# A change to the first stage of a causal-attention and gated feed-forward kernel: a small constant, two low halves, column sums and transposes are placed elsewhere

## The chip, the cores and the metric

One core of one Trainium2 chip. The metric is the device time of one execution in microseconds. Below, TensorE is PE in the rows (PEld is its weight load), VectorE DVE, ScalarE ACT, GpSimd POOL and SyncE SP.

## What is computed

Causal attention over 4 batches, 12 heads, 448 positions and a head width of 64, then an RMS norm and a gated feed-forward layer over the 1792 tokens (768 columns, 1536 inner columns), all in float32:

```python
scores = np.where(mask, -1e9, q @ k.T / sqrt(64))
attn = np.exp(scores - np.max(scores, axis=-1, keepdims=True))
attn = attn / (np.sum(attn, axis=-1, keepdims=True) + 1e-09)
x = (attn @ v)                       # heads side by side: 1792 x 768
xn = x / np.sqrt(np.mean(x * x, axis=-1, keepdims=True) + 1e-06) * rms_g
g = xn @ w_gate
out = (g * sigmoid(g) * (xn @ w_val)) @ w_out
```

## The kernel before, in words

The tokens are handled in three groups. The work of attention comes in units: one pair of heads, and 256 queries for the first group. The first group has 12 units (`ENDS[0]`), two for each of the six chunks c of 128 columns of x. This first stage, some 60 us, is where everything below happens; later stages do the same for the other groups while the feed-forward layer of the group before runs on TensorE.

Every matrix product of the feed-forward layer is made of three matmuls in a short float format: weights and x are split into a high half (ScalarE's cast, `w_h` in L456, `xh` in L362) and a low half (what the cast left off, `w_l` in L458 on VectorE or through `pool_op`, L105, on GpSimd; `xl` in L363). A weight chunk is such a triple on one column chunk: L502, L503, L504. Weight tiles arrive as 64-bit words and are converted first: ScalarE in L443, then VectorE in L444 and L446.

The order on each engine is the order in which the program is written; each engine works its queue strictly in turn. The program is written tick by tick: `round_steps(p)` gives six steps for round p, and each step is a tick. Scores of unit p + 3 (`DP`), products of unit p and transposes of unit p + 1 belong to round p. `post(delay, f)` puts f so many ticks later; the delays stand in the table `T`. `LOAD`, `CONVERT` and `SPLIT` give the ticks at which weight tiles 0 to 7 are loaded, converted and split, and `READY_W`, `READY_X` those from which weight chunks may be woven in.

For one unit: scores on TensorE (L195), row minimum and mask on VectorE (L204), exponentials with their row sums on ScalarE (L207, four of them), the constant 1e-9 added to the sums on ScalarE (L229), reciprocal on VectorE (L216), the rows scaled on GpSimd (L212, four instructions; on ScalarE in L210 for the last unit), transposes on TensorE in two halves e = 0 and 1 (L251), their copies to SBUF (L255 on VectorE, L257 on ScalarE), products with v (L280).

After the second unit of a chunk: the split of x, and its squares on ScalarE (L318). The tile `sq` has one buffer; chunks 1 to 4 are added on GpSimd into `acc` (L105). For the last chunk the sum over columns is made by `column_sums` on TensorE: first of `acc`, then of `sq`, into the same bank (L371, four matmuls of one column each time). `rms_first` then makes the square root on ScalarE (L380), the reciprocal and four diagonal blocks on VectorE (L383, L385), and a matmul that spreads them (L389), copied on ScalarE (L390). The first eviction of a product (L519) needs that. The stage ends with the scores of the next group (`refill`).

## Time and profile before

| | us |
|---|---|
| median of 3 runs (669.01 to 669.62) | 669.44 |
| the profiled execution | 670.19 |
| its span, first to last instruction | 668.4 |
| TensorE busy (98% of the span) | 657.7 |
| VectorE busy (77%) | 515.3 |
| ScalarE busy (54%) | 360.9 |
| GpSimd busy (44%) | 291.3 |

The shares are means over stages that differ much. Three views tell of the first stage: busy time by stretch, the chain of waits (the work that ended last, followed back from the end, in order of time), and each engine's instructions in order of time. In the last, an instruction's duration can be longer than the time till the next one starts, since they overlap a little.

### The profile page before, as it was taken

To read this page: it belongs to the slowest core of one execution; us is meant where nothing else is said; L and a number is where in the kernel's file an instruction comes from. 1 tells how busy PE (TensorE), PEld (TensorE's weight loads), DVE (VectorE), ACT (ScalarE), POOL (GpSimd) and SP (SyncE) were. 2 spreads that over 40 slices of the span, in tenths; PEclk is the share of its full clock that TensorE was granted. 3 is DMA by queue.
4 is the path that set the end of the run, shared out by engine and by line. 5 is a ranking of instruction groups with operands and counts; after the bars stand their busy time and mean duration, and the time that the engine had idled before them with its cause. 6 is when DMAs were issued, how large, how long until landed. Compare 5 with 4: busy or idle time off the path is not lost.

```text
span 668.4 us, 11848 instructions
## 1 busy us (share of the span) xinstructions
PE 657.7 (98%) x4122; PEld 551.7 (83%) x4122; DVE 515.3 (77%) x1049; ACT 360.9 (54%) x801; POOL 291.3 (44%) x278
## 2 busy tenths in 40 slices
PE   9899999999999999999999999999999999999997
PEld 6567877778777777777777778888899999999997
DVE  5997987889876776778778885496776866889992
ACT  6996866766866445454454444435424343355540
POOL 4670313245344365766767475643424342502220
PEclk9999999999999999999999999999999999999999
DMA  8876888898696375866757555235576467562641
GB/s 258 288 254 217 252 284 266 257 293 244 220 353 234 118 218 192 272 203 222 239 190 253 167 180 181 91 112 187 206 245 190 155 210 236 196 173 69 179 143 60
DMA packets 71357, 138.81 MB, mean 208 GB/s; under 512 B 7745, under 2 KB 39233, under 8 KB 71297
## 3 DMA queue, kind: packets, MB, share of 16 engines
q1 hardware_dynamic: 71296, 138.05, 63.4%
q8 instruction: 33, 0.54, 0.3%
q14 instruction: 28, 0.22, 0.1%
HBM read 104.21 MB, written 33.82 MB: 206 GB/s over the span
## 4 chain that ended last, share of the span: by engine, by line
PE 86%; ACT 5%; DVE 3%; DMA 3%; issue 2%; POOL 1%; SPq 0%; DVEq 0%; ACTq 0%
PE m_ps L502 14%; PE m_ps L504 14%; PE m_ps L503 13%; PE s_ps L652 9%; PE m_ps L652 8%; PE a_ps L280 6%; PE t_ps L251 5%; PE y_ps L652 5%; PE x_ps L652 4%; PE s_ps L195 4%; PE x_ps L195 2%; ACT sp L207 2%; DMA w<-in_w 1%; DVE a_l L545 1%; DMA v_r<-in_v 1%
## 5 line engine op out<-in xcount | busy, mean ns | idle before, releaser
L212 POOL TENSOR_SCALAR sp<-sp,rs 128x384 f32<-128x384 f32 (+3 forms) x164 | 122.9, 769 | 164.0 <-DVE rs L216 151.1
L502 PE MATMUL m_ps<-xh,w_h 128*128 128x512 f32 x276 | 116.8, 423 | 0.0
L207 ACT ACTIVATE sp<-sp,nm 128x128 f32<-128x128 f32 (+3 forms) x168 | 87.1, 522 | 42.8 <-DVE nm L204 42.8
L504 PE MATMUL m_ps<-xh,w_l 128*128 128x512 f32 x276 | 108.5, 393 | 0.0
L503 PE MATMUL m_ps<-xl,w_h 128*128 128x512 f32 x276 | 108.0, 391 | 0.0
L105 POOL TENSOR_TENSOR a_l<-w_q,a_h 128x768 fp32r<-128x768 f32 x24 | 48.2, 2010 | 82.4 <-ACT a_h L543 81.0
L255 DVE COPY pt<-t_ps 128x384 f32<-128x384 f32 (+1 forms) x79 | 46.7, 591 | 24.1 <-PE t_ps L251 23.7
L504 PEld LDWEIGHTS m_ps<-xh,w_l 128*128 128x128 f32 x276 | 51.8, 188 | 11.6
L502 PEld LDWEIGHTS m_ps<-xh,w_h 128*128 128x128 f32 x276 | 51.9, 188 | 11.3 <-issue 3.0
L105 POOL TENSOR_TENSOR w_l<-w_r,w_h 128x768 fp32r<-128x768 f32 x30 | 57.6, 1926 | 6.3 <-ACT w_h L456 6.0
L503 PEld LDWEIGHTS m_ps<-xl,w_h 128*128 128x128 f32 x276 | 52.2, 189 | 8.1 <-issue 0.2
L502 PE MATMUL m_ps<-hh,w_h 128*128 128x512 f32 x144 | 58.1, 403 | 0.0
L251 PE MATMUL t_ps<-ident,sp 128*128 128x128 f32 (+1 forms) x348 | 56.5, 274 | 0.6 <-ACT pt L257 0.5
L251 PEld LDWEIGHTS t_ps<-ident,sp 128*128 128x128 f32 (+1 forms) x348 | 42.9, 138 | 16.5 <-issue 2.4
L504 PE MATMUL m_ps<-hh,w_l 128*128 128x512 f32 x144 | 56.2, 390 | 0.0
L503 PE MATMUL m_ps<-hl,w_h 128*128 128x512 f32 x144 | 56.1, 390 | 0.0
L280 PEld LDWEIGHTS a_ps<-pt,v_r 128*64 128x64 f32 (+1 forms) x816 | 37.2, 137 | 19.7 <-issue 8.4
L204 DVE CUSTOM_DVE_ANT_0 sp<-s_ps,mask 128x128 f32<-128x128 f32 (+2 forms) x114 | 42.6, 422 | 11.1 <-PE s_ps L195 9.7
L280 PE MATMUL a_ps<-pt,v_r 112*64 112x64 f32 (+2 forms) x816 | 47.3, 262 | 1.4 <-DVE pt L255 1.2
L543 ACT CAST a_h<-w_q 128x768 fp32r<-128x768 f32 (+1 forms) x48 | 35.0, 753 | 13.2 <-DMA w_q<-wz 4.9
L105 POOL TENSOR_TENSOR acc<-acc,sq 128x384 f32<-128x384 f32 (+1 forms) x19 | 22.5, 1185 | 39.5 <-ACT sq L340 36.7
L458 DVE TENSOR_TENSOR w_l<-w_c,w_h 128x768 fp32r<-128x768 f32 x36 | 37.5, 1042 | 0.6 <-ACT w_h L456 0.5
(196 smaller groups left out, 1620.5 us busy)
## 6 DMA issues: line engine op xcount, KB each, us to landing
w<-in_w SPq DMA_DIRECT2D x36, 768.0 KB, 5.1
w<-w_c SPq DMA_DIRECT2D x36, 384.0 KB, 5.6
w_r<-w SPq DMA_DIRECT2D x36, 384.0 KB, 4.6
qk_r<-in_qk SPq DMA_DIRECT2D x48, 256.0 KB, 4.4
qk_r<-in_qk SPq DMA_DIRECT2D x12, 512.0 KB, 6.4
v_r<-in_v SPq DMA_DIRECT2D x12, 448.0 KB, 4.2
v_r<-in_v SPq DMA_DIRECT2D x24, 192.0 KB, 3.0
wy<-w_r SPq DMA_DIRECT2D x24, 192.0 KB, 3.9
```

What stands on the lines that cost most here:

```text
L105: nc.gpsimd.tensor_tensor(out_, a, b, op=op)
L195: nc.tensor.matmul(ps, r[:, q0: q0 + nq], r[:, k0: k0 + wd], start=True, stop=True)
L204: nc.vector.tensor_tensor_reduce(out=sp, in0=ps, in1=mk, scale=nsc, scalar=3.0e38, op0=ALU.add, op1=ALU.min, accum_out=nm)
L207: post(T["exp" if p >= ENDS[0] else "exp0"], lambda: nc.scalar.activation(sp, sp, AF.Exp, bias=nm, scale=-1.0, accum_out=sm))
L212: pr["norms"].append(lambda: nc.gpsimd.tensor_scalar(sp, sp, rs, 1.0, op0=ALU.mult, op1=ALU.mult))
L251: nc.tensor.transpose(ps[:kb, at: at + P], pr["sp"][e][:, o + kb * j: o + kb * (j + 1)], ident)
L255: nc.vector.tensor_copy(pt[:kb, :at], ps[:kb, :at])
L280: nc.tensor.matmul(at_[e * D: (e + 1) * D, p % 2, q0: q0 + n], raw_v[p][:kb, h, j, e, :], pr["pt", e][:kb, a0: a0 + n], start=(j == 0), st ...
L502: nc.tensor.matmul(ps, wh[:, k, :], mh, start=(first and k == ks[0]), stop=False)
L503: nc.tensor.matmul(ps, wh[:, k, :], ml, start=False, stop=False)
L504: nc.tensor.matmul(ps, wl[:, k, :], mh, start=False, stop=(last and k == 5))
L652: nc.tensor.matmul(ps, a[x], b[y], start=first and n == 0, stop=last and n == 2, skip_group_check=True)
```

## The change

Five edits, all in the first stage:

- The constant 1e-9 is added to the row sums on VectorE, just ahead of the reciprocal, for the first 12 units; ScalarE's addition (L229) stays for later ones.
- The copy of the first half of the transposes (e = 0) goes to VectorE for units 0, 2, 4, 6, 8 rather than for units 0, 1, 3, 4, 6, 7, 9; the others go to ScalarE.
- The last chunk's squares are added into `acc` by VectorE, and `column_sums` runs once, three ticks after the squares rather than one (`r0`).
- The low halves of weight tiles 0 and 1 are made by GpSimd rather than VectorE.
- In the last round that still makes scores (p = 8) both halves of the transposes follow each other, rather than three ticks apart.

```diff
-         ld=4, ld1=11, lv=2, norm0=7, norm=6, norm1=2, r0=1, sq=1, ...
+         ld=4, ld1=11, lv=2, norm0=7, norm=6, norm1=2, r0=3, sq=1, ...
         def norm():
+            if p < ENDS[0]:
+                nc.vector.tensor_scalar_add(pr["sm"][:, :nb], pr["sm"][:, :nb], 1e-9)
             nc.vector.reciprocal(pr["rs"][:, :nb], pr["sm"][:, :nb])
...
-            post(T["exp" if p >= ENDS[0] else "exp0"], lambda: nc.scalar.activation(
-                pr["sm"][:, :nb], pr["sm"][:, :nb], AF.Identity, bias=tiny))
+            if p >= ENDS[0]:
+                post(T["exp"], lambda: nc.scalar.activation(
+                    pr["sm"][:, :nb], pr["sm"][:, :nb], AF.Identity, bias=tiny))
...
-            if kind or p < ENDS[0] and (e or p % 3 < 2 and p < 10):
+            if kind or p < ENDS[0] and (e or p % 2 == 0 and p < 10):
                 nc.vector.tensor_copy(pt[:kb, :at], ps[:kb, :at])
...
         def squares():
-            if last:
-                cols = column_sums(acc[0, 0], None, True)
             nc.scalar.activation(sq, x, AF.Square)
             if last:
-                post(T["r0"], lambda: rms_first(column_sums(sq, cols, False)))
+                nc.vector.tensor_tensor(acc[0, 0], acc[0, 0], sq, op=ALU.add)
+                post(T["r0"], lambda: rms_first(column_sums(acc[0, 0])))
...
-                             start=first and i == 0, stop=not first, skip_group_check=True)
+                             start=True, stop=True)
...
-            if s < NU or s > NU + 2 * NF and s % 2:
+            if 1 < s < NU or s > NU + 2 * NF and s % 2:
...
-        if s_:
+        if s_ and p + DP < ENDS[0] - 1:
             return [scores, products, ts[0]] + 2 * noop + ts[1:]
```

What this does to the order at three places. On VectorE, at the end of the first stage, from the last low halves of x (`xl`) to the first eviction (`gr`); `rc` is the reciprocal root, `dg` the diagonal blocks, `w_c` a converted weight tile. Before:

```order
L363 SCALAR_TENSOR_TENSOR xl<-a_ps,g_sb,xh 128x512
L363 SCALAR_TENSOR_TENSOR xl<-y_ps,g_sb,xh 128x512
L383 RECIPROCAL rc<-rc 128x4
L385 TENSOR_SCALAR dg<-ident,rc 128x128 x4
L444 TENSOR_SCALAR w_717<-w_717 128x768
L446 SCALAR_TENSOR_TENSOR w_c<-w_c,w_717 128x768
L444 TENSOR_SCALAR w_820<-w_820 128x768
L446 SCALAR_TENSOR_TENSOR w_c<-w_c,w_820 128x768
L519 TENSOR_TENSOR gr<-m_ps,rms 128x512
```

After:

```order
L365 SCALAR_TENSOR_TENSOR xl<-a_ps,g_sb,xh 128x512
L321 TENSOR_TENSOR acc<-acc,sq 128x512
L365 SCALAR_TENSOR_TENSOR xl<-y_ps,g_sb,xh 128x512
L446 TENSOR_SCALAR w_716<-w_716 128x768
L448 SCALAR_TENSOR_TENSOR w_c<-w_c,w_716 128x768
L446 TENSOR_SCALAR w_819<-w_819 128x768
L448 SCALAR_TENSOR_TENSOR w_c<-w_c,w_819 128x768
L385 RECIPROCAL rc<-rc 128x4
L387 TENSOR_SCALAR dg<-ident,rc 128x128 x4
L521 TENSOR_TENSOR gr<-m_ps,rms 128x512
```

The addition of the squares is new, and the four instructions of the weight conversions now stand ahead of the reciprocal and the diagonal blocks.

On TensorE, at the same place, from the last column sums (`t_ps<-ones`) to the spread (`t_ps<-dg`). Before:

```order
L371 MATMUL t_ps<-ones,sq 128x1 x4
L502 MATMUL m_ps<-xh,w_h 128x512
L503 MATMUL m_ps<-xl,w_h 128x512
L504 MATMUL m_ps<-xh,w_l 128x512
L502 MATMUL m_ps<-xh,w_h 128x512
L503 MATMUL m_ps<-xl,w_h 128x512
L504 MATMUL m_ps<-xh,w_l 128x512
L502 MATMUL s_ps<-xh,w_h 128x512
L503 MATMUL s_ps<-xl,w_h 128x512
L504 MATMUL s_ps<-xh,w_l 128x512
L389 MATMUL t_ps<-dg,ones 128x512
```

After:

```order
L373 MATMUL t_ps<-ones,acc 128x1 x4
L504 MATMUL s_ps<-xh,w_h 128x512
L505 MATMUL s_ps<-xl,w_h 128x512
L506 MATMUL s_ps<-xh,w_l 128x512
L391 MATMUL t_ps<-dg,ones 128x512
```

Two of the three weight chunks between the sums and the spread now stand ahead of the sums.

On GpSimd, in the middle of the stage, from the end of unit 6's scaling over unit 7's (`sp_531`, `sp_532` before, `sp_530`, `sp_531` after) to the addition of chunk 1's squares. Before:

```order
L212 TENSOR_SCALAR sp_476<-sp_476,rs_474 128x256
L212 TENSOR_SCALAR sp_531<-sp_531,rs_530 128x128
L212 TENSOR_SCALAR sp_531<-sp_531,rs_530 128x256
L212 TENSOR_SCALAR sp_532<-sp_532,rs_530 128x128
L212 TENSOR_SCALAR sp_532<-sp_532,rs_530 128x256
L105 TENSOR_TENSOR acc_406<-acc_406,sq_515 128x512
```

After:

```order
L212 TENSOR_SCALAR sp_476<-sp_476,rs_474 128x256
L105 TENSOR_TENSOR w_l_573<-w_c_399,w_h_572 128x768
L212 TENSOR_SCALAR sp_530<-sp_530,rs_529 128x128
L212 TENSOR_SCALAR sp_530<-sp_530,rs_529 128x256
L212 TENSOR_SCALAR sp_531<-sp_531,rs_529 128x128
L212 TENSOR_SCALAR sp_531<-sp_531,rs_529 128x256
L105 TENSOR_TENSOR acc_405<-acc_405,sq_515 128x512
```

The low half of weight tile 1 stands between unit 6's scaling and unit 7's; that of tile 0 stands likewise between units 4 and 5.

## Rows read from the trace of the kernel before

**Rows 1.** The page's first part: busy us (share) x instructions.

```profile
PE 657.7 (98%) x4122; PEld 551.7 (83%) x4122; DVE 515.3 (77%) x1049; ACT 360.9 (54%) x801; POOL 291.3 (44%) x278
```

**Rows 2.** Busy time by stretch: length, engines, granted clock, DMA share, GB/s.

```profile
17.00:30.00 13.00, 11.07 (x83) 7.46 (x82) 11.70 (x46) 12.87 (x44) 8.26 (x14) 1.00 0.78 279
30.00:43.00 13.00, 12.38 (x87) 8.38 (x85) 12.75 (x43) 12.48 (x40) 10.97 (x15) 1.00 0.80 274
43.00:50.30 7.30, 6.71 (x42) 4.74 (x42) 5.72 (x10) 7.24 (x20) 3.91 (x6) 1.00 0.74 250
50.30:60.00 9.70, 9.70 (x53) 7.60 (x53) 6.13 (x12) 6.01 (x10) 0.00 (x0) 1.00 0.50 177
60.00:80.00 20.00, 20.00 (x96) 15.84 (x96) 19.27 (x41) 15.47 (x35) 4.22 (x4) 1.00 0.80 264
...
663.00:668.40 5.40, 1.84 (x11) 1.53 (x9) 0.56 (x1) 0.00 (x0) 0.00 (x0) 0.95 0.20 73
```

**Rows 3.** The chain of waits, 27 to 35 us: start, us, what.

```profile
27.76 0.37 ACT pt L257
...
29.88 0.02 issue
29.91 0.30 ACT sm L229
30.20 0.73 ACT w_h L456
30.93 2.37 POOL sp L212 x3
33.30 1.27 POOL acc L105
...
34.59 0.60 ACT sq L318
```

**Rows 4.** Groups by line and shape, 17 to 50 us: busy us, mean ns, idle before.

```profile
L229 ACT ACTIVATE sm<-sm,tiny 128x4 f32<-128x4 f32 x8 | 2.4, 298 | 0.3
...
L216 DVE RECIPROCAL rs<-sm 128x4 f32<-128x4 f32 x8 | 1.4, 172 | 1.6 <-ACT sm L229 1.5
```

**Rows 5.** The same view of the whole span, GpSimd: low halves of later weight tiles.

```profile
L105 POOL TENSOR_TENSOR w_l<-w_r,w_h 128x768 fp32r<-128x768 f32 x30 | 57.6, 1926 | 6.3 <-ACT w_h L456 6.0
```

**Rows 6.** GpSimd in order of time: start, us, first shape of four instructions.

```profile
9.19 1.64 POOL L212 TENSOR_SCALAR sp<-sp,rs 128x128 f32<-128x128 f32 x4 [6.42 <-DVE rs L216]
...
30.58 2.72 POOL L212 TENSOR_SCALAR sp<-sp,rs 128x128 f32<-128x128 f32 x4 [0.99 <-DVE rs L216]
```

**Rows 7.** TensorE in order of time; each fp32 matmul counts twice.

```profile
50.26 0.87 PE L280 MATMUL y_ps<-pt,v_r 128*64 128x256 f32 x8 [0.18 <-ACT pt L257]
51.06 1.05 PE L371 MATMUL t_ps<-ones,acc 128*128 128x1 f32 x8
...
55.72 1.02 PE L389 MATMUL t_ps<-dg,ones 128*128 128x512 f32 x2
...
60.12 0.37 PE L195 MATMUL s_ps<-qk_r 64*128 64x128 f32 x1
```

**Rows 8.** ScalarE in order of time: the last chunk's squares.

```profile
51.70 0.58 ACT L318 ACTIVATE sq<-y_ps 128x512 f32<-128x512 f32 x1
```

**Rows 9.** VectorE in order of time: a conversion at 41.41, then the stage's end.

```profile
41.41 1.48 DVE L446 SCALAR_TENSOR_TENSOR w_c<-w_c,w 128x768 int32<-128x768 int32 x1
...
52.89 0.75 DVE L363 SCALAR_TENSOR_TENSOR xl<-y_ps,g_sb,xh 128x512 fp32r<-128x512 f32 x1 [2.96 <-ACT xh L362]
54.03 0.18 DVE L383 RECIPROCAL rc<-rc 128x4 f32<-128x4 f32 x1 [0.39 <-ACT rc L380]
...
55.13 0.56 DVE L444 TENSOR_SCALAR w<-w 128x768 int32<-128x768 int32 x1
...
57.19 0.96 DVE L446 SCALAR_TENSOR_TENSOR w_c<-w_c,w 128x768 int32<-128x768 int32 x1
58.07 0.68 DVE L519 TENSOR_TENSOR gr<-m_ps,rms 128x512 f32<-128x512 f32 x1
```

More of the change, by code (lines that the diff above doesn't have):

```diff
@@ L46 @@
 T = dict(c0=0, c2=4, c20=16, c3=4, c30=18, c26=5, c36=5, c5=6, c50=19, c56=7, exp=1, exp0=3, gt=1, hh=1, hl=4, ws=5, ld2=7,
-         ld=4, ld1=11, lv=2, norm0=7, norm=6, norm1=2, r0=1, sq=1, acc=10, acc4=7, dg=1, spread=3, r1=5, so=3, wl=2, wl0=8, wl2=5, wl4=1, xl=2, xl0=9)
+         ld=4, ld1=11, lv=2, norm0=7, norm=6, norm1=2, r0=3, sq=1, acc=10, acc4=7, dg=1, spread=3, r1=5, so=3, wl=2, wl0=8, wl2=5, wl4=1, xl=2, xl0=9)
 LOAD = (1, 15, 27, 37, 48, 60, 72, 84)
@@ L365, in x_split, with column_sums @@
         xh[b, c], xl[b, c] = h, l
-    def column_sums(sq, ps, first):
-        ps = bank("t")[:, : W // P] if first else ps
+    def column_sums(sq):
+        ps = bank("t")[:, : W // P]
         for i in range(W // P):
             nc.tensor.matmul(ps[:, i: i + 1], sq[:, P * i: P * (i + 1)], ones[:, :1],
-                             start=first and i == 0, stop=not first, skip_group_check=True)
+                             start=True, stop=True)
         return ps
```

## The prediction

> **What bounds the kernel now.** I read the page's first part, then busy time by stretch. TensorE is busy 98% of the span [rows 1]. From 60 us on it has no gap to speak of: 20.00 of 20.00 us in the first stretch behind the first stage [rows 2]. So what delays or advances TensorE before 60 us moves the end by as much, unless a later stretch takes it back. The change lies wholly before 60 us. There, from 30 to 43 us, VectorE (12.75 of 13.00), ScalarE (12.48) and GpSimd (10.97) are all nearly full, and TensorE has small gaps [rows 2]. The chain of waits in that stretch runs over ScalarE, except where it goes to GpSimd: ScalarE casts the high half of weight tile 1 until 30.93, GpSimd scales the rows of unit 7 and adds the squares of chunk 1 to the running sum, and only at 34.59 can ScalarE take the next square, since the tile `sq` has one buffer [rows 3]. From 50.3 to 60 us TensorE is full (9.70 of 9.70) [rows 2]: it alternates column sums, the matmul that spreads 1/rms, and weight chunks of three matmuls. The time to predict is therefore two terms: when the product of the last unit of the first stage starts (50.26 now [rows 7]), and how long it takes from there to the spread (55.72 now [rows 7]).
>
> **Part 1: until the last product at 50.26.** The additions of the small constant: eight lie between 17 and 50 us, 298 ns each [rows 4]; in the chain one takes 0.32 us of ScalarE, from the start of the 0.02 gap at 29.88 to the cast at 30.20 [rows 3]. On VectorE no row shows an addition to 128x4; the reciprocal of the same shape, 172 ns [rows 4], is nearest, so it costs between 0 and 0.17, and I take 0.17. The copies of transposed probabilities: in this stretch units 3, 7 and 9 come to ScalarE at 0.37 each [rows 3] and unit 8 leaves it. ScalarE alone would thus be earlier by 8 x 0.32 - 2 x 0.37 = 1.8 us at 50.26. VectorE loses two copies and two low halves and gains the additions, so it isn't the engine that keeps this back.
>
> GpSimd is. It gets two low halves of 128x768; the same operation takes it 1926 ns in the mean of 30 later ones [rows 5]. The second stands in its queue behind the cast on ScalarE and ahead of unit 7's scaling and chunk 1's addition, which is just where the chain runs now. Step by step: four additions are gone ahead of the cast and one copy is new (unit 3), so the cast ends at 30.93 - 4 x 0.32 + 0.37 = 30.0. GpSimd then makes the low half, to 31.9. The scaling follows: 2.72 as at 30.58, or 1.64 as at 9.19, where VectorE had little to do [rows 6], so to 33.6 or 34.6. The addition of 1.27 [rows 3] ends at 34.8 to 35.9. ScalarE's next square starts there, against 34.59 now: 0.2 to 1.3 later. (If GpSimd held nobody, ScalarE would be there 5 x 0.32 - 0.37 = 1.2 earlier.) From that square to 50.26 three more additions go and one more copy comes than goes: 0.6 earlier. So the product starts between 1.8 us earlier (GpSimd never in the way) and 0.7 later. I take **0.0**, near the middle of GpSimd's own two values (0.4 earlier, 0.7 later), because the rows of this stretch stand nearer to 2.72 than to 1.64. The transposes side by side let the two copies of unit 9 start before the two weight chunks; what this gives TensorE is swallowed at 50.26, since that product waits for ScalarE's queue, where the table load and the last copy stand.
>
> The row beside this: VectorE's conversion at 41.41 took 1.48 us while GpSimd was at work, against 0.96 for the same at 57.19 [rows 9]. The Trainium skill's "SBUF — State Buffer" (section "SBUF: two separate sides") says that GpSimd shares a port pair with VectorE instructions that read two inputs from SBUF, that whoever starts first holds it for its whole instruction, and that the other is blocked till then. By it a low half on GpSimd can hold a conversion for up to 1.9 us where this row shows 0.5 more; by it the product would start up to 1.4 us later, once for each of the two halves.
>
> **Part 2: from the last product to the spread.** TensorE's own work shrinks by one block of column sums, 1.05 us from first start to last end [rows 7], some 0.9 of it by itself. But the spread now waits. VectorE's queue before: reciprocal at 54.03, four diagonal blocks, then two weight conversions of two instructions each, from 55.13 to 58.07 [rows 9]. After: both conversions stand **ahead of** the reciprocal, and TensorE's queue has one weight chunk instead of three between the column sums and the spread. Walked from the product at 50.26 with the old durations: ScalarE's square runs at 51.70 for 0.58 [rows 8], to 52.3; VectorE adds it to the sum, which no row shows: between the 0.56 of a one-input instruction on 128x768 at 55.13 [rows 9] and the 0.75 of a two-input one at 52.89 on the same 128x512 [rows 9]; I take 0.6, to 52.9; then the low half of x, 0.7, to 53.6; the two conversions, 58.07 - 55.13 = 2.9, to 56.5; reciprocal and diagonal, 55.13 - 54.03 = 1.1, to 57.6; with the hand-over the spread starts at 57.7 instead of 55.72, so **2.0 later**. TensorE reaches it at about 54.8 (55.72 less 0.9) and has nothing else in its queue: it stands still for some 2.9 us, which eats the block saved and more. Who waits behind it: the weight chunks, then the scores at 60.12 [rows 7]. The longer delay of the column sums themselves, two steps, costs nothing: VectorE's sum is there when TensorE has done its three chunks. DMA issues and SyncE's queue keep their order.
>
> **The sum.** 0.0 + 2.0 = 2.0 us later at the scores at 60.12, and TensorE is full behind them. The profiled execution took 670.19 us (span 668.4), 0.75 above the median of 669.44. So 672.2 profiled, and **671.4** in the median. What a measurement tells from no change is about 0.2%, 1.3 us: 668.1 to 670.8 counts as the same.
>
> **Rivals.**
> 1. *GpSimd is not in the way.* The ScalarE time freed comes through: the product starts 0.7 to 1.8 earlier. For it: GpSimd has gaps in 17 to 30 us, and POOL spans are rough. Against: the chain passes over it in just the row where the new work goes [rows 3]. Time: 2.0 - 1.3 = 0.7 later, 670.1.
> 2. *TensorE's clock falls in the stall.* The granted clock is 1.00 in every stretch but the last, 663 to 668.4, where it is 0.95; there TensorE had done its last matmul and idled [rows 2]. A stall of 2.9 us has no like in this trace before that. If the grant falls from 2.4 to 1.2 GHz, each us of TensorE's work costs one more until it rises; the work from the spread at 55.72 to the scores at 60.12 is some 4 us [rows 7], so 0 to 4 more; I take 2, 673.4. The Trainium skill's "TensorE: Matmul & The Clock Gate" (section "What's actually happening") states such a fall to half rate when the engine idles. Only the last stretch agrees; whether 2.9 us suffices no row shows.
> 3. *Faster.* All idle time of TensorE between 17 and 50 us goes (13.00 - 11.07, 13.00 - 12.38 and 7.30 - 6.71, 3.1 us [rows 2]) and the stretched matmuls beside it with it, so that the product starts over 3.3 us earlier; from there on the gain outweighs the 2.0 by more than the 1.3. At 4 us earlier: 667.4. Against: it is twice what ScalarE gives up.
> 4. *GpSimd holds more.* Both low halves block a conversion as the row at 41.41 hints, and the product starts 1.3 later: 672.7.
>
> **How the numbers follow.** Forecast 0.52, rival 1 0.20, rival 2 0.17, rival 3 0.05, rival 4 0.06. The low end, 669.6, takes in most of rival 1; the high end, 673.5, rival 4 and the middle of rival 2. Outside lie rival 3, the best of rival 1 and the longer half of rival 2, under 0.2 together. Slower by over 0.2%: rivals 2 and 4 and all but 0.03 of the forecast, 0.72. Same: 0.23. Faster: 0.05.
>
> **What would show it.** The last product of the first stage within 0.6 us of 50.26. The reciprocal of rc behind four conversion instructions at about 56.5, and TensorE idle for 2 to 4 us before a spread at about 57.7, with VectorE named as the releaser. Scores of the refill at about 62.1. ScalarE's square of chunk 2 still released by GpSimd's addition at about 35. Wrong would be a product before 48.5, or a spread without a gap before it; a granted clock below 1.00 between 55 and 65 us speaks for rival 2.

## The result, and the profile after

| | before | after |
|---|---|---|
| median of 6 runs each, us | 669.23 (668.22 to 670.51) | 675.34 (673.04 to 677.30) |
| ratio, 95% interval | | 1.0093 [1.0074, 1.0113] |
| the profiled execution, us | 670.19 | 673.04 |
| its span, us | 668.4 | 670.5 |

The change made the kernel slower by 6.1 us, three times the 2.0 that were forecast (671.4 against 669.44), and outside the range. The profiled execution of after is the fastest of its six. Two executions on record, 924.74 us of the kernel before and 1306.16 us of h1 below, lie far above all others of their kernels and are in no ratio.

TensorE in order of time, after (start, us, what; in brackets the idle time before and who ended it), against [rows 7]. Unit 8's scores come first, then the last product of the first stage, column sums, spread, scores of the next group:

```profile
28.20 0.93 PE L195 MATMUL s_ps<-qk_r 64*128 64x128 f32 x8
...
52.25 0.87 PE L283 MATMUL y_ps<-pt,v_r 128*64 128x256 f32 x8
...
55.23 0.95 PE L373 MATMUL t_ps<-ones,acc 128*128 128x1 f32 x8
...
59.74 1.10 PE L391 MATMUL t_ps<-dg,ones 128*128 128x512 f32 x2 [2.74 <-DVE dg L387]
...
64.21 0.37 PE L195 MATMUL s_ps<-qk_r 64*128 64x128 f32 x1
```

The last product is 2.0 later (52.25 against 50.26), where the prediction had 0.0. From it to the spread are 7.49 us against 5.46, 2.0 more, as forecast, and the 2.74 us of idle time are new. The next group's scores are 4.1 later.

VectorE at the same place, after, against [rows 9]:

```profile
55.58 0.55 DVE L446 TENSOR_SCALAR w<-w 128x768 int32<-128x768 int32 x1
56.17 0.96 DVE L448 SCALAR_TENSOR_TENSOR w_c<-w_c,w 128x768 int32<-128x768 int32 x1
57.05 0.55 DVE L446 TENSOR_SCALAR w<-w 128x768 int32<-128x768 int32 x1
57.63 0.96 DVE L448 SCALAR_TENSOR_TENSOR w_c<-w_c,w 128x768 int32<-128x768 int32 x1
58.51 0.17 DVE L385 RECIPROCAL rc<-rc 128x4 f32<-128x4 f32 x1
58.72 0.88 DVE L387 TENSOR_SCALAR dg<-ident,rc 128x128 f32<-128x128 f32 x4
```

Four conversion instructions stand ahead of the reciprocal, and TensorE waits for what comes behind it. Busy time by stretch, after (length, then PE, PEld, DVE, ACT, POOL, granted clock, DMA share, GB/s), against [rows 2]:

```profile
30.00:43.00 13.00, 12.25 (x85) 8.39 (x85) 12.90 (x47) 9.99 (x32) 10.18 (x15) 1.00 0.79 269
43.00:52.30 9.30, 8.67 (x49) 5.48 (x47) 8.00 (x13) 8.32 (x22) 5.29 (x7) 1.00 0.64 211
52.30:60.00 7.70, 4.96 (x29) 3.72 (x30) 5.17 (x11) 2.82 (x5) 0.00 (x0) 1.00 0.57 208
```

From 30 to 43 us ScalarE is 2.5 us less busy than before (9.99 against 12.48), and yet nothing got earlier: VectorE is at 12.90 of 13.00. Its small additions are the odd rows. VectorE, after, one instruction of a weight conversion, then four of the twelve additions:

```profile
24.45 1.61 DVE L446 TENSOR_SCALAR w<-w 128x768 int32<-128x768 int32 x1
...
30.54 1.69 DVE L217 TENSOR_SCALAR sm<-sm 128x4 f32<-128x4 f32 x1
...
34.91 0.94 DVE L217 TENSOR_SCALAR sm<-sm 128x4 f32<-128x4 f32 x1
...
42.77 0.86 DVE L217 TENSOR_SCALAR sm<-sm 128x4 f32<-128x4 f32 x1
...
46.38 1.08 DVE L217 TENSOR_SCALAR sm<-sm 128x4 f32<-128x4 f32 x1 [0.57 <-ACT sp L207]
```

GpSimd in order of time, after, at the same moments:

```profile
23.83 1.82 POOL L105 TENSOR_TENSOR w_l<-w_c,w_h 128x768 fp32r<-128x768 f32 x1 [1.23 <-ACT w_h L458]
...
30.38 1.83 POOL L105 TENSOR_TENSOR w_l<-w_c,w_h 128x768 fp32r<-128x768 f32 x1 [0.52 <-ACT w_h L458]
...
34.54 1.29 POOL L105 TENSOR_TENSOR acc<-acc,sq 128x512 f32<-128x512 f32 x1
...
42.32 1.28 POOL L105 TENSOR_TENSOR acc<-acc,sq 128x512 f32<-128x512 f32 x1
...
46.15 1.28 POOL L105 TENSOR_TENSOR acc<-acc,sq 128x512 f32<-128x512 f32 x1
```

Each of the four additions ends within 0.04 us of the GpSimd instruction that was running when it began: 30.54 + 1.69 = 32.23 and 30.38 + 1.83 = 32.21; 35.85 and 35.83; 43.63 and 43.60; 47.46 and 47.43. Of the other eight, seven take 0.16 to 0.18; the one at 11.00 takes 0.24 and ends 0.02 behind a scaling of GpSimd (9.60 + 1.62 = 11.22). The conversion instruction, which takes 0.55 at 55.58, takes 1.61 beside the low half of tile 0.

Two things remain unclear from this. The five other executions of after took 1.4 to 4.3 us more than the profiled one, at a mean granted clock of 0.997 (0.999 in the profiled one, 1.000 before). And the end of the profiled execution is only 2.1 later than before's, though the scores at 64.21 were 4.1 late. The second is answered by the first experiment.

### The profile page after: what moved, and what is told of

The parts are those of the page before. It is cut to its first block, busy times and chain, and to the rows that moved or that the text cites. A ratio compares the mean times of both kernels' runs of the same rounds, so it can differ in the third digit from the quotient of the medians.

```text
span 670.5 us, 11846 instructions
## 1 busy us (share of the span) xinstructions
PE 658.0 (98%) x4114; PEld 551.1 (82%) x4114; DVE 516.7 (77%) x1058; ACT 358.3 (53%) x791; POOL 292.5 (44%) x280
## 4 chain that ended last, share of the span: by engine, by line
PE 89%; DVE 3%; ACT 2%; DMA 2%; issue 2%; POOL 2%; SPq 0%; POOLq 0%; DVEq 0%; ACTq 0%
PE m_ps L504 14%; PE m_ps L506 14%; PE m_ps L505 13%; PE s_ps L654 10%; PE m_ps L654 9%; PE a_ps L283 6%; PE y_ps L654 5%; PE t_ps L254 5%; PE x_ps L654 4%; PE s_ps L195 4%; PE x_ps L195 2%; POOL sp L212 1%; DMA w<-in_w 1%; ACT sp L207 1%; PE m_ps L863 1%
## 5 line engine op out<-in xcount | busy, mean ns | idle before, releaser
L212 POOL TENSOR_SCALAR sp<-sp,rs 128x384 f32<-128x384 f32 (+3 forms) x164 | 120.4, 752 | 165.0 <-DVE rs L218 143.2
L195 PE MATMUL s_ps<-qk_r 64*128 64x128 f32 (+3 forms) x252 | 36.8, 433 | 0.0
```

What stands on the lines that cost most here:

```text
L195: nc.tensor.matmul(ps, r[:, q0: q0 + nq], r[:, k0: k0 + wd], start=True, stop=True)
L212: pr["norms"].append(lambda: nc.gpsimd.tensor_scalar(sp, sp, rs, 1.0, op0=ALU.mult, op1=ALU.mult))
```

## The experiments

The time of the same instruction shifts by up to a microsecond between executions, so the table gives distances between instructions of one trace, all from TensorE in order of time: from unit 6's scores to unit 8's (a), from there to the last product (b), from that to the spread (c), from the spread to the next group's scores (d). Before: 19.00, 27.08, 50.26, 55.72, 60.12. The kernels ran on several chips, so ratios to the kernel before on the same chip are compared.

| kernel | a | b | c | d | mean clock, all executions | ratio to before |
|---|---|---|---|---|---|---|
| before | 8.08 | 23.18 | 5.46 | 4.40 | 0.999 to 1.000 | 1 |
| before again (x_before) | 7.93 | 23.18 | 5.48 | 4.40 | 1.000 | |
| after | 8.96 | 24.05 | 7.49 | 4.47 | 0.997 to 0.999 | 1.0093 [1.0074, 1.0113] |
| after again (h4) | 8.98 | 24.05 | 7.49 | 6.10 | 0.995 to 0.997 | 1.0091 [1.0077, 1.0104] |
| e1: constant back on ScalarE | 8.85 | 24.41 | 7.49 | 5.99 | 0.995 to 0.997 | 1.0091 [1.0078, 1.0104] |
| e9: addition in the form with a sum | 7.81 | 23.43 | 7.48 | 6.14 | 0.994 to 0.999 | 1.0072 [1.0054, 1.0090] |
| e10: idle time filled | 8.03 | 24.06 | 7.41 | 4.49 | 1.000 | 1.0052 [1.0040, 1.0064] |
| e12: conversions late | 8.06 | 24.06 | 5.49 | 4.47 | 0.999 to 1.000 | 1.0025 [1.0015, 1.0034] |
| f1: late, form with a sum | 7.81 | 23.41 | 5.51 | 4.47 | 0.999 to 1.000 | 1.0020 [1.0010, 1.0030] |
| f2: late, low halves back | 7.74 | 24.36 | 5.52 | 4.46 | 0.999 to 1.000 | 1.0019 [1.0010, 1.0027] |
| f3: late, both | 7.38 | 23.65 | 5.50 | 4.47 | 0.998 to 1.000 | 1.0014 [1.0006, 1.0023] |
| e4: before + column sums | 8.10 | 23.30 | 7.50 | 6.06 | 0.994 to 0.997 | 1.0058 [1.0046, 1.0071] |
| e5: before + addition | 8.20 | 24.53 | 5.47 | 4.40 | 0.999 to 1.000 | 1.0024 [1.0013, 1.0034] |
| g3: before + addition with a sum | 7.94 | 23.71 | 5.46 | 4.40 | 0.999 to 1.000 | 1.0010 [1.0001, 1.0019] |
| g1: g3 + transposes side by side | 8.20 | 23.70 | 5.46 | 4.40 | 0.999 to 1.000 | 1.0011 [1.0002, 1.0020] |
| h1: before, no addition | 7.54 | 23.07 | 5.47 | 4.39 | 0.999 to 1.000 | 0.9992 [0.9983, 1.0001] |
| h2: before + low halves | 9.29 | 23.77 | 5.47 | 4.40 | 0.999 to 1.000 | 1.0038 [1.0025, 1.0052] |
| h3: h1 + low halves | 8.38 | 22.65 | 5.47 | 4.39 | 0.999 to 1.000 | 1.0003 [0.9994, 1.0012] |

### The kernel before once more (x_before)

No edit.

> The kernel before, unchanged: a second trace of it, because products of the first stage lay 0.6 to 1.4 us apart in executions of kernels that are alike up to there (50.89 and 51.47 where only what follows differs, against 52.25). If the start is what varies, the distance from the scores of unit 3 to the last product is 39.0 +- 0.3 us here again (11.25 to 50.26), whatever both are by themselves, and the changed kernel's first stage is about 0.7 longer (39.7 in the two kernels that are like it up to there). If the distance is 39.5 or more here, the first stage isn't longer at all, and the 2.0 us by which the product came late in the profiled execution are chance.

Measured from unit 3's scores, as the expectation has it, the distance is 38.49 (11.46 to 49.95), 0.2 under what the expectation allowed, against 39.01 in the first trace of before, and 39.70 and 39.68 in the two kernels that are like the changed one up to there (e12 and e10). That stretch still holds waits for loads that differ between executions; the part from unit 8's scores on (column b) is the same in both traces of before, 23.18, and 24.05 or 24.06 in all four of the changed program. So the first stage is longer, by 0.88 in b. In a, two executions of the changed program have 8.03 and 8.06, as before, and two have 8.96 and 8.98. In those two, ScalarE stood waiting for the words of a weight tile. ScalarE in order of time, after:

```profile
17.16 0.94 ACT L445 ACTIVATE w_c<-w 128x768 f32<-128x768 f32 x1 [1.03 <-DMA w<-in_w]
```

In h4's trace it waited 1.60 for the same, in e12's 0.15, in e10's not at all. The 2.0 of the profiled execution are thus 0.9 in b, which belong to the change, 0.9 in a, which go with a late load, and 0.2 ahead of both.

A late load alone doesn't cost so much. ScalarE, f2 (below), where a is 7.74:

```profile
17.15 0.93 ACT L445 ACTIVATE w_c<-w 128x768 f32<-128x768 f32 x1 [1.18 <-DMA w<-in_w]
```

GpSimd, e12:

```profile
22.46 1.81 POOL L105 TENSOR_TENSOR w_l<-w_c,w_h 128x768 fp32r<-128x768 f32 x1 [1.09 <-DVE rs L218]
```

f2 makes no low half of tiles 0 and 1 on GpSimd. In after that of tile 0 waits for ScalarE's cast and starts 4.6 behind unit 6's scores (23.83 against 19.24), in e12 3.7 behind them (22.46 against 18.77), and GpSimd's scaling stands behind it in the queue. So in these traces the late load seems to pass through the low half; no run tests it, and whether the change makes late loads likelier, four traces can't say.

The apparent gain behind 400 us is no gain of after's. Busy time of the profiled execution of before, in this stretch:

```profile
400.00:500.00 100.00, 98.46 (x559) 85.68 (x558) 69.16 (x105) 41.53 (x73) 46.88 (x33) 1.00 0.51 171
```

TensorE stood still for 1.5 us there in that execution. In x_before it was busy 99.86 of 100, in after 99.81, and the span of x_before is 666.1. Nothing was given back; the profiled execution of before was a long one. From the next group's scores to the end of the span thirteen of the eighteen traces have 606.3 to 606.5 us, e9's has 607.1, and those of before, f1, f2 and h3, which all have this standstill, 608.3 or 608.4. A ratio can hold a part of these 2.0 us that no column shows.

### The idle time ahead of the spread: e12, e10, e4, and after again

In e12 the two conversions stand behind the diagonal blocks, and nothing else moves:

```diff
-c26=5, c36=5, ... c56=7
+c26=8, c36=8, ... c56=10
```

> The changed kernel with VectorE's four conversion instructions of weight tiles 5 and 6 posted three ticks later, so that they stand behind the reciprocal and the four diagonal blocks; nothing else moves. Theory: they alone make the stall. The product stays at 52.2, the spread starts 4.6 to 5.2 us behind it instead of 7.49, TensorE's gap ahead of it is under 0.5 us, and the scores of the next group start 2.3 to 2.8 earlier than 64.21. If TensorE's clock falls because of the stall in most executions of the changed kernel (mean 0.997), it is 1.000 here in all, and the median falls by 4 to 5 us, to about 671. If the clock has nothing to do with the stall, it stays at 0.997 in most and the median falls by some 2.5 us or less. Rival: the spread waits for something else as well (the square, the sum, the root), and comes no earlier than 58.5.

TensorE, e12:

```profile
50.89 0.87 PE L283 MATMUL y_ps<-pt,v_r 128*64 128x256 f32 x8
...
53.86 0.95 PE L373 MATMUL t_ps<-ones,acc 128*128 128x1 f32 x8
...
56.38 1.10 PE L391 MATMUL t_ps<-dg,ones 128*128 128x512 f32 x2 [0.77 <-DVE dg L387]
```

The spread comes 5.49 behind the product, a little later than the 4.6 to 5.2 expected and with a gap of 0.77 rather than under 0.5, but as early as in before (5.46); the clock is 0.999 or 1.000 in all ten executions, and 4.4 us of the 6.1 are gone (1.0091 to 1.0025). In e10 the idle time stays but is filled:

```diff
             ps = bank("t")
+            for _ in range(12):
+                nc.tensor.matmul(ps[:, :P], ones, ones, start=True, stop=True)
             nc.tensor.matmul(ps, ones, dg, start=True, stop=True)
```

> The changed kernel with 12 matmuls of 128x128 (ones by ones, into the bank that the spread overwrites, 0.23 us each as at the kernel's start) in TensorE's queue just ahead of the spread: TensorE works through most of the 2.74 us in which it stood still, and waits for no less. Theory (the idle stretch makes the clock fall in most executions): spread and scores start where they did within 0.3 us, the mean clock is 1.000 in all executions, and the median falls by about 2 to 4 us from 675.3. Rival (the longer time of most executions comes from elsewhere, as a gain behind 400 us that they miss): clock and median as in the changed kernel.

The spread is as late as in after (7.41 behind the product), yet the clock is 1.000 in all five, and the ratio 1.0052. So of after's 6.1 us, 1.0025 to 1.0052 is the wait (669.70 to 671.72 on one chip, 2.0 us), and 1.0052 to 1.0091 or 1.0093, some 2.7 us (the two intervals together leave about 1.4 to 3.8), goes with TensorE standing idle meanwhile. After again:

> The changed kernel as it is, beside the others on one chip. By the sum of what the runs showed (0.9 us from unit 8's scores to the last product, 2.0 from there to the spread, and the clock at half for some 3 us behind the stall in most executions, 1.5 to 3 us): ratio 1.007 to 1.010, mean clock 0.994 to 0.998 in most executions; where the profiled one falls, granted clock near 0.5 from the end of the stall on, spread to the scores of the next group 5.5 to 6.2 instead of 4.47. If the clock stays at 1.000 in all on this chip: ratio 1.004 to 1.0055.

This time the profiled execution has the fall. Busy time by stretch, after again (the clock is the third number from the right):

```profile
58.00:60.00 2.00, 0.00 (x0) 0.00 (x0) 1.93 (x6) 0.00 (x0) 0.00 (x0) 1.00 0.58 232
60.00:62.00 2.00, 1.87 (x3) 0.86 (x4) 0.00 (x0) 0.00 (x0) 0.00 (x0) 0.52 1.04 318
62.00:64.00 2.00, 2.00 (x7) 1.63 (x6) 0.44 (x1) 1.50 (x3) 0.00 (x0) 0.62 1.02 346
64.00:66.00 2.00, 2.00 (x10) 1.53 (x9) 1.24 (x3) 1.99 (x3) 0.00 (x0) 1.00 0.69 277
```

The same stretch of e10:

```profile
58.00:60.00 2.00, 2.00 (x12) 1.35 (x11) 0.82 (x4) 0.00 (x0) 0.00 (x0) 1.00 0.88 280
60.00:62.00 2.00, 2.00 (x11) 1.61 (x10) 1.20 (x2) 1.94 (x3) 0.00 (x0) 1.00 0.95 341
```

TensorE idles to 60.13, and as it starts again the grant is at 0.5 (1.2 of 2.4 GHz) until about 63.5; spread to scores take 6.10 instead of 4.47, 1.6 us lost in this execution, and 1.5 to 1.7 in those of e1, e4 and e9. So the slow stretch itself costs 1.6 in the traces, and the 2.7 of the medians hold something else as well. Between the two traces compared here the scores lie 2.86 apart (66.23 and 63.37), of which 1.2 arise ahead of the last product, 0.95 of them in column a. Whether the medians differ for the same reason is not shown. In after's first trace an idle time of the same length (2.74 against 2.76) was followed by a grant of 1.00. The fall is not certain, then; the mean clock, 0.997 or less in all other executions of the changed kernel, says that it came in most. The Trainium skill's "TensorE: Matmul & The Clock Gate" (section "What's actually happening") states the fall to half rate of an idle engine; four of the five traces with this gap agree (h4, e1, e4 and e9). The column-sum edit alone, on the kernel before (e4), is enough:

```diff
-r0=1
+r0=3
...
-                cols = column_sums(acc[0, 0], None, True)
...
-                post(T["r0"], lambda: rms_first(column_sums(sq, cols, False)))
+                nc.vector.tensor_tensor(acc[0, 0], acc[0, 0], sq, op=ALU.add)
+                post(T["r0"], lambda: rms_first(column_sums(acc[0, 0])))
...
```

> The kernel before with the column-sum edit alone (VectorE adds the last squares, one block of sums, three ticks later); constant, copies, low halves and transposes as before. Theory (stall and clock come from this edit by itself): unit 3's scores to the last product as before (38.5 to 39.0), product to spread 7.4 to 7.6 instead of 5.46, a gap of 2 to 3 us ahead of it that VectorE's diagonal ends, mean clock below 0.999 in most executions; ratio 1.003 with the clock steady, 1.005 to 1.007 with it falling in most. Rival (the stall needs the other edits, because the conversions come late only with them): product to spread under 6.5, ratio within 1.002.

TensorE, e4:

```profile
50.45 0.87 PE L280 MATMUL y_ps<-pt,v_r 128*64 128x256 f32 x8 [0.21 <-ACT pt L257]
...
57.95 1.10 PE L388 MATMUL t_ps<-dg,ones 128*128 128x512 f32 x2 [2.76 <-DVE dg L384]
...
64.01 0.37 PE L195 MATMUL s_ps<-qk_r 64*128 64x128 f32 x1
```

Gap and slow stretch (6.06 from spread to scores) are there, at 3.9 us (1.0058) without any of the other edits. The columns add up to that: c is 2.0 longer than before, d 1.7, b 0.1.

### The additions held by GpSimd: e9, e5, g3, f1

e9 leaves the addition in its place, in another form of the same instruction:

```diff
-nc.vector.tensor_scalar_add(pr["sm"][:, :nb], pr["sm"][:, :nb], 1e-9)
+nc.vector.tensor_scalar(pr["sm"][:, :nb], pr["sm"][:, :nb], 1e-9, None,
+                        op0=ALU.add, op1=ALU.add, accum_out=pr["nm"][:, :1])
```

> The changed kernel with the small addition left on VectorE at its place, but in the form that also writes a sum of its results (one more column of 128x1, which nothing reads). The Trainium skill's SBUF — State Buffer, section on who interferes with whom, says that the plain form can take the port pair shared with GpSimd and that the form with the sum can't; no run so far shows it. Theory (the addition is held by a port that its form wants): all additions take about 0.2 us, GpSimd busy or not, the product starts 1 to 3.5 us earlier than 52.25, and the time falls by as much. Rival 1 (any VectorE instruction is held beside GpSimd): the additions stay at 0.9 to 1.7 us and the time too. Rival 2 (the low halves on GpSimd set the product): additions at 0.2, product within 0.5 us of 52.25, time unchanged.

One line's instructions, after (min/median/max ns):

```profile
L217 DVE TENSOR_SCALAR sm<-sm x12: 160/174/1693, 9.0 to 46.4; 128x4 f32<-128x4 f32 x12
```

The same line in e9 (its second instruction writes the sum):

```profile
L217 DVE TENSOR_SCALAR_CACHE_REDUCE sm<-sm x12: 146/152/160, 9.0 to 45.0; 128x4 f32<-128x4 f32 x12
L217 DVE DVE_READ_ACCUMULATOR sm<-sm x12: 77/83/92, 9.1 to 45.1; 128x1 f32 x12
```

No addition is held any more, b is 0.63 shorter and the time 1.3 to 1.4 us, though the intervals of 1.0072 and 1.0091 overlap. Rival 1 of the expectation falls: it is the form that is held, not whatever stands beside GpSimd. The Trainium skill's "SBUF — State Buffer" (section "Who interferes with whom") says so: copies, casts and the plain form of this instruction can take the port pair that GpSimd needs, the form that writes its sum can't; the rows of the two forms agree. Of the 3.9 us that the four holds add (1.69, 0.94, 0.86 and 1.08, less 0.17 each), b shows only 0.6. One reason stands in the rows: the conversion right behind a held addition finds GpSimd done and takes 0.93 (at 43.76 of after), where it took 1.48 before [rows 9] and takes 1.37 in e9 (at 41.72). The addition alone, on the kernel before, is the first edit of the change in e5, and with e9's form in g3:

```diff
+            if p < ENDS[0]:
+                nc.vector.tensor_scalar_add(pr["sm"][:, :nb], pr["sm"][:, :nb], 1e-9)
...
-            post(T["exp" if p >= ENDS[0] else "exp0"], lambda: nc.scalar.activation(
+            if p >= ENDS[0]:
+                post(T["exp"], lambda: nc.scalar.activation(
```

> The kernel before with the constant's addition alone moved to VectorE, in its plain form. Theory (it is held while GpSimd scales rows or adds squares, with no low half there): of the eight additions between 17 and 50 us two to four take 0.7 to 1.3 us; ScalarE is relieved of eight times 0.30; unit 3's scores to the last product 38.5 to 39.5, ratio 0.999 to 1.0015. Rival (only the low halves on GpSimd hold it): all additions at 0.2, the product 1 us or more earlier than before (distance 37.7 or less), ratio 0.997 to 0.999.

> The kernel before with the constant's addition moved to VectorE in the form that also writes a sum, and nothing else: the same as the kernel with the addition alone but for the form. Theory: no addition over 0.2 us, unit 3's scores to the last product 0.5 to 1 us shorter than with the plain form, 37.7 to 38.5, ratio 0.998 to 1.000. Rival (off the path here, since ScalarE and the later weight chunks set the product): the same as with the plain form within 0.2 us.

VectorE, e5:

```profile
34.59 0.87 DVE L217 TENSOR_SCALAR sm<-sm 128x4 f32<-128x4 f32 x1
...
42.48 0.96 DVE L217 TENSOR_SCALAR sm<-sm 128x4 f32<-128x4 f32 x1
...
46.00 1.26 DVE L217 TENSOR_SCALAR sm<-sm 128x4 f32<-128x4 f32 x1
```

GpSimd, e5:

```profile
34.14 1.29 POOL L105 TENSOR_TENSOR acc<-acc,sq 128x512 f32<-128x512 f32 x1
...
42.12 1.29 POOL L105 TENSOR_TENSOR acc<-acc,sq 128x512 f32<-128x512 f32 x1
...
45.97 1.27 POOL L105 TENSOR_TENSOR acc<-acc,sq 128x512 f32<-128x512 f32 x1
```

No low half is on GpSimd here, and three additions are held all the same, to the end of GpSimd's own additions. b grows by 1.35 in e5 and by 0.53 in g3; 669.88 and 668.87 are the medians on one chip, 1.0 us apart. Both are worse than expected: e5 had 1.0015 as its upper end and is at 1.0024, and even where the addition is not held, the move costs 0.1% (1.0010), where g3's expectation had 0.998 to 1.000. f1 is e9's edit and e12's together:

> The changed kernel with the conversions of tiles 5 and 6 behind the diagonal blocks (so that no stall moves the clock) and the small addition in the form that also writes a sum. Against the kernel with the late conversions alone, ratio 1.0025 to before. Theory (the held additions cost the first stage about 0.9 us): unit 3's scores to the last product 38.8 instead of 39.7, ratio 1.0010 to 1.0015. Rival (what an addition waits is made up elsewhere): ratio 1.0025 again, within 0.0007.

b is 23.41 against e12's 24.06, 0.65 shorter. The ratio (1.0020 against 1.0025) is too coarse to show it; it lies in the range of the expectation's rival, and f1's trace is one of the four with the standstill behind 400 us.

### What ScalarE's relief is worth: h1

On the kernel before:

```diff
-            post(T["exp" if p >= ENDS[0] else "exp0"], lambda: nc.scalar.activation(
-                pr["sm"][:, :nb], pr["sm"][:, :nb], AF.Identity, bias=tiny))
+            if p >= ENDS[0]:
+                post(T["exp"], lambda: nc.scalar.activation(
+                    pr["sm"][:, :nb], pr["sm"][:, :nb], AF.Identity, bias=tiny))
```

> The kernel before without the constant's addition in the first 12 units: neither ScalarE nor VectorE does it (this leaves a part of the computation out). The stretch from unit 8's scores to the last product is 23.2 us in the kernel before. If ScalarE sets it, as the prediction had it, it shortens by 0.8 us or more (five additions of 0.30 lie in it, and more ahead), and the ratio is 0.9975 to 0.999. If VectorE sets it, it stays within 0.3 us of 23.2, and the ratio is 0.9992 to 1.0005.

b is 23.07, 0.11 less than before, and a some 0.4 to 0.5 less. Busy time by stretch, h1:

```profile
30.00:43.00 13.00, 12.00 (x85) 8.02 (x83) 12.83 (x42) 10.71 (x37) 11.54 (x17) 1.00 0.77 267
```

ScalarE has 1.8 us less to do there than before (10.71 against 12.48), VectorE is as full (12.83). What ScalarE does with the time, h1:

```profile
33.77 0.60 ACT L321 ACTIVATE sq<-a_ps 128x512 f32<-128x512 f32 x1 [1.49 <-POOL acc L105]
```

GpSimd, h1:

```profile
29.77 2.72 POOL L212 TENSOR_SCALAR sp<-sp,rs 128x128 f32<-128x128 f32 x4 [0.99 <-DVE rs L218]
```

ScalarE waits for GpSimd (1.49, and 0.72 at its next square; 0.18 and 0.24 before), and GpSimd waits for VectorE's reciprocal exactly as before, 0.99 [rows 6]. The theory that ScalarE set this stretch falls. That VectorE's time counts there is shown by g3 against h1: the two differ by the twelve additions on VectorE alone, 0.15 and 0.08 each and none held, and a and b together are 1.04 longer in g3 (31.65 against 30.61); the ratios, 1.0010 and 0.9992, agree, with intervals that just touch.

### The low halves: e1, f2, f3, h2, h3

e1 is the changed kernel with the constant back on ScalarE:

```diff
-            if p < ENDS[0]:
-                nc.vector.tensor_scalar_add(pr["sm"][:, :nb], pr["sm"][:, :nb], 1e-9)
...
-            if p >= ENDS[0]:
-                post(T["exp"], lambda: nc.scalar.activation(
+            post(T["exp" if p >= ENDS[0] else "exp0"], lambda: nc.scalar.activation(
```

> The changed kernel with one edit undone: the constant goes back to ScalarE (eight additions of about 0.30 us until the last product). Theory: in the changed kernel VectorE's small additions were held while GpSimd worked (0.9 to 1.7 us instead of 0.17), and this is what made the last product of the first stage start at 52.25 instead of 50.26. Then the product starts here at 50.3 to 51.2, with the reciprocals at 0.17 each, the stall ahead of the spread stays at 2 to 3 us, and the time falls by 1 to 2 us against the changed kernel. Rival: GpSimd's two low halves made the product late by themselves, and the held additions cost nothing. Then the product stays within 0.5 us of 52.25, and the time is that of the changed kernel within 1 us.

The time doesn't fall (1.0091), and the product starts at 51.75: the theory fails, and the rival's two numbers came. But b grows from 24.05 to 24.41, so taking the additions away didn't leave the rest as it was. With the constant on ScalarE and the low halves on GpSimd another wait takes over; h2, the low halves alone on the kernel before, shows it by itself:

```diff
-            if s < NU or s > NU + 2 * NF and s % 2:
+            if 1 < s < NU or s > NU + 2 * NF and s % 2:
```

> The kernel before with the low halves of weight tiles 0 and 1 alone moved to GpSimd. If VectorE sets the stretch, it loses 0.94 us there for one of them (the other lies ahead of it) and may be held on a conversion for up to 1 us: unit 8's scores to the last product 22.9 to 23.2, ratio 0.999 to 1.0005. If GpSimd's queue sets it (scaling of unit 7 behind the low half), 23.5 to 24.2 and ratio 1.0005 to 1.002.

GpSimd, h2:

```profile
31.19 1.82 POOL L105 TENSOR_TENSOR w_l<-w_c,w_h 128x768 fp32r<-128x768 f32 x1 [1.10 <-ACT w_h L456]
32.99 1.93 POOL L212 TENSOR_SCALAR sp<-sp,rs 128x128 f32<-128x128 f32 x4
34.89 1.97 POOL L105 TENSOR_TENSOR acc<-acc,sq 128x512 f32<-128x512 f32 x1
```

ScalarE, h2:

```profile
36.90 0.60 ACT L318 ACTIVATE sq<-a_ps 128x512 f32<-128x512 f32 x1 [2.33 <-POOL acc L105]
```

The low half stands ahead of unit 7's scaling, the scaling ahead of chunk 1's addition, and ScalarE waits 2.33 us for its end, at 36.90 where it was 34.59 [rows 3]. GpSimd's addition itself takes 1.97 there, 1.27 in [rows 3]; VectorE's conversion of 34.55 to 35.73 ran when it began. Columns a and b together grow by 1.8 to 1.95, the time by 2.5 us (1.0038), worse than either side of its expectation. With the additions gone from ScalarE (h3) the same low halves cost little:

> The kernel before without the constant's addition in the first 12 units (this leaves a part of the computation out) and with the low halves of weight tiles 0 and 1 on GpSimd: ScalarE and VectorE both relieved. If the two engines set the stretch in turn, so that either relief alone is lost, it shortens here by more than the two changes did one by one: 22.2 to 22.7, ratio 0.997 to 0.999. If not, it is what the better of the two gave, within 0.2 us.

b is in the expected range (22.65), but a + b is 31.03 against h1's 30.61 and before's 31.11 to 31.26, and the ratio, 1.0003, is one that can't be told from before: relieving both engines gains no more than relieving one. With the constant on VectorE, f2 is e12 without the edit of the low halves, and f3 is f1 without it:

> The changed kernel with the conversions of tiles 5 and 6 behind the diagonal blocks, and the low halves of weight tiles 0 and 1 back on VectorE; the additions stay in the plain form. Theory (GpSimd's low halves stand 1.8 us each ahead of unit 5's and unit 7's scaling and hold a conversion to 1.5 us and an addition to 1.7 us): unit 3's scores to the last product 38.7 to 39.2 instead of 39.7, ratio 1.0008 to 1.0018 against 1.0025. Rival (GpSimd has room for them, and VectorE's 0.94 us for each costs as much): 1.0025 or more.

> Both together: conversions of tiles 5 and 6 behind the diagonal blocks, the addition in the form that also writes a sum, and the low halves of tiles 0 and 1 on VectorE. If the held additions and the low halves are two costs, they add up: unit 3's scores to the last product 38.0 to 38.5, ratio 0.9985 to 1.0005, and this is the first version that is no slower than the kernel before. If both are one cost (the additions are held by the low halves), the result is that of the better of the two alone, 1.0010 to 1.0015.

Taking the low halves back moves a + b from 32.12 to 32.10 (e12 to f2) and from 31.22 to 31.03 (f1 to f3): b is 0.2 to 0.3 longer, a 0.3 to 0.4 shorter. In the changed kernel, then, the low halves cost next to nothing where no load is late; by the distance the rival of f2's expectation was right, while the ratio (1.0019) lies between the two. f3 comes out as its expectation had it for one cost, not two. It is the best of the versions that keep the column sums, and still 0.14% slower than before, though its columns add up to 41.00, no more than before's (40.99 and 41.12); where these 0.9 us lie, its trace doesn't show.

### The transposes side by side: g1

g3 and one edit more:

```diff
-        if s_:
+        if s_ and p + DP < ENDS[0] - 1:
```

> The kernel before with two edits: the addition on VectorE in the form that also writes a sum, and the transposes of the last round that still makes scores side by side. Against the kernel with the addition alone: if the transposes side by side are worth anything, the last product starts 0.2 to 0.6 us earlier after the product before it, ratio 0.997 to 0.999; if that product waits for ScalarE's queue all the same (the table load and the last copy), no difference, within 0.0005.

b is 23.70 against g3's 23.71 and the ratio the same: nothing, as the prediction said. The copies of transposed probabilities were not tried alone. No version that computes everything beat the kernel before.

## Why the prediction was right or wrong

- **From the last product to the spread: right.** 2.0 forecast, 2.03 measured, with the reciprocal behind four conversion instructions and the gap as drawn (2.9 forecast, 2.74). e12 and e4 show that the queue order on VectorE alone makes it.
- **The price of the idle time: the first step that failed.** The sum let TensorE stand still for 2.9 us and then go on at full speed: the clock was a term put at nothing, and stood only in rival 2, with a chance of 0.17 and 2 us, as a case in the forecast's place. It came beside the forecast. The slow stretch costs 1.6 us in the traces that have it, up to 2.7 in the medians, and e10 shows that the idle time of TensorE causes it. The sign that the prediction named for it, a grant below 1.00 between 55 and 65 us, is missing in after's first trace and there in h4's. The row that spoke for it, 0.95 in the last stretch [rows 2], held the longest idle time in the trace. It should have been the likelier case, since the forecast itself put an idle time nearly as long into the first stage.
- **Until the last product: the second step that failed.** It was put at 0.0, at most 0.7 late. It is 0.9 late by the change, 2.0 in the profiled execution. Two terms were mis-sized. The first: ScalarE's relief was counted as up to 1.8 us earlier, with the sentence that VectorE "isn't the engine that keeps this back". h1 gives the relief with nothing in return and gains 0.5 to 0.7 in a and b, and ScalarE spends the rest waiting for GpSimd, which waits for VectorE. The row against it stood in [rows 2], VectorE at 12.75 of 13.00, and was read and passed over because the chain of waits ran over ScalarE and GpSimd. The second: an addition on VectorE was bounded by 0 and 0.17 from the reciprocal of the same shape [rows 4]. It took 0.86 to 1.69 four times between 30 and 48 us. The reciprocal was the nearest row in shape and not in kind: in no trace here is it held in the first stage (0.16 to 0.18, as at 34.07 of before, while GpSimd's addition of 33.27 to 34.56 ran), while the plain addition is. The prediction weighed the port that GpSimd and VectorE share, but only for instructions with two inputs from SBUF.
- **The chain over GpSimd: a true mechanism, in the wrong kernel.** The low half ahead of unit 7's scaling does delay ScalarE's square, by 2.3 us in h2. In after it is 35.86 against 34.59, inside the forecast 0.2 to 1.3 later, but f2 shows that it is not what makes the product late there. Rival 1 is out, since nothing came earlier. What rival 4 describes is there for one of the two low halves (the conversion of 1.61 at 24.45), but f2, which has no low half on GpSimd there, is no shorter in a + b than e12 (32.10 and 32.12).
- **The range** ended at 673.5, since the cases were treated as exclusive. They add up. Against x_before the scores of the next group come 6.4 later in h4's trace, and the span is 6.4 longer (672.6 against 666.1): 0.9 in b, 2.0 in c, 1.7 in d, 1.05 in a with its late load, and 0.8 ahead of unit 6's scores, which the change doesn't explain. The sign was right, and the chance of slower, 0.72, would have been higher with the clock.

## What to carry to other kernels

When work goes from one full engine to another, the busy time of the receiver in that stretch is the first number to read: ScalarE at 12.48 of 13.00 was relieved and VectorE at 12.75 paid (g3 against h1). An instruction of 0.17 us can cost a microsecond beside GpSimd, and which form it has decides it, so bound a new instruction by rows of the same kind, not of the same size. A forecast that leaves TensorE idle for some 3 us ahead of a stage in which it is the bound has to carry the price of a slower clock behind it as a term of its sum, or something to fill the gap.

## What the runs showed of the hardware

- A plain addition of a constant to 128x4 on VectorE was held to within 0.04 us of the end of GpSimd's running instruction, whether that was a subtraction of 128x768 (1.69 us) or an addition of 128x512 (0.86 to 1.26). The plain one-input conversion of 128x768 was held as well (1.61 instead of 0.55), the reciprocal of 128x4 was not (0.16 to 0.18). In the form that also writes a sum it took 0.15 every time, plus 0.08 for the sum.
- After 2.74 to 2.76 us without a matmul TensorE's grant was 0.5 for some 3 us in four of the five traces that have that gap (h4, e1, e9, e4), and 1.00 in the fifth (after). Twelve matmuls that compute nothing removed the fall: 671.72 where the idle version had a ratio that makes 674.3 on that chip.
- Executions of one program differ by some 0.9 us in the first stage (column a, 8.03 to 8.98 for the changed one), and of these four the later ones are those in which ScalarE waited over 1 us for a weight tile; behind it by 2.0 us (606.3 or 608.3 from the next group's scores to the end).
